# Banded attention output in 64x64 tiles, a re-weighted list schedule, and a reordered first MLP batch

## The chip, the cores and the metric

The kernel runs on one core of one Trainium2 chip. The metric is device time in microseconds (us) of one execution; times given for a kernel are the median of several runs on the chip. The trace is of one profiled execution.

## The reference, cut to what matters

Three stages follow each other on an activation of 4 batches x 576 tokens x 512 channels, all in float32.

```python
# 1. attention over (4, 8 heads, 576, 64): a pooled and a local part, added
q_d, k_d, v_d = mean of q, k, v over groups of 4 tokens         # 144 pooled tokens
out_up = repeat(softmax(q_d @ k_d.T / 8) @ v_d, 4)
mask = abs(pos[:, None] - pos[None, :]) < 4                     # a band of 7 tokens
out_local = softmax(where(mask, q @ k.T / 8, -1e9)) @ v
x = out_up + out_local                                          # heads side by side: 512 channels
# 2. gated MLP with spatial mixing
h = gelu(x @ w_in); u, v = halves of h
v_n = layernorm(v) * g_ln
x = x + (u * (w_sg @ v_n + b_sg)) @ w_out
# 3. four attention experts (causal), top 2 of 4 mixed per token, then the output projection
```

The inputs w_in and w_out arrive as float64 words and are converted to float32 pairs (a high and a low part) on the chip.

## The kernel before, in words

**Stage 1** (function `phase1`) works on 16 units u, each a pair of heads of one batch. The unit's steps carry the names of the list in `unit`:

- `lq`, `lk`, `lv`, `lw`: loads of q, k, v and of ten 64-token windows of v. A q or k load is "whole" (one DMA, six tokens of a head in a run) or split per head (two DMAs of 64-element runs); the table `WHOLE` says for which units.
- `Aq`, `Ak` (TensorE, PE) turn q and k, `aq`, `ak` (ScalarE, ACT) copy them out of PSUM as `qT`, `kT`; `aqd`, `akd` add four neighbouring tokens (VectorE, DVE).
- `Bm` writes the band mask into PSUM, `Bs` adds the local scores (20 matmuls in 64x64 tiles), `Bd` makes the pooled scores. `xm`, `xs`, `sx` (DVE) and `ex` (ACT) are the local softmax, `ym` (DVE) and `ey` (ACT) the pooled one, `n` (DVE) the reciprocals, `ny`, `nx` (GpSimd, POOL) the normalisation, `V` (POOL) the pooled v.
- `Cc`, `Ca` turn the weights, `cb`, `ca` copy them out. `Do` is the banded output: ten matmuls a unit, each with a 128x128 stationary tile `vw` in which the two heads stand on the diagonal and the rest is zero. `Du` is the pooled output; `du` and `dx` add both into `xT`.

The order on every engine is fixed when the program is built: class `Steps` holds each step's engine and cost, its dependencies and a wanted time; `run` takes, among the steps that could start within `NEAR` of the earliest on an engine, the one with the earliest wanted time. PE pays `DRAIN` where a step's tile shape (`mode`) differs from the last one's. An engine executes its list strictly in that order.

Beside the units the same list holds eight conversions of w_in (`conv_job`: a 512 KB load, four DVE operations, one on ACT, three on POOL), five transposes of w_sg (`w_sg_job`), the split of batch 0 into high and low parts (`xhi`, `xlo`) and the first MLP product `du` of batch 0, which is the last thing in it.

**Stage 2** (`phase2`) takes the batches in turn: `dv(b)` (value half, per tile of 128 tokens: PE, then gelu on ACT, `bn_stats` on DVE, the power -0.5 on POOL, the scaling on DVE, and a split on ACT and POOL), `e(b)` (spatial mixing), `dv(b+1)`, `du(b+1)`, `f(b)`. Batch 0's `e` does three column blocks over the first three tiles before it comes to the last ones. Four conversions of w_out run beside it. **Stage 3** (`phase3`) is the mixture of experts; its code is not touched.

Of the kernel before, what the change touches and what calls it, by code (L numbers as in the profile page):

```python
# [8 lines left out]
F32 = mybir.dt.float32  # L9
F32R = mybir.dt.float32r  # L10
# [14 lines left out]
class Steps:  # L25
# [6 lines left out]
    NEAR = 0.4  # L32
# [30 lines left out]
    def run(self):  # L63
        while self.todo:
            can = []
            for name, (engs, fn, want, deps, ring, readers, mode) in self.todo.items():
                t = self.ready(name)
                if t is None:
                    continue
                for e in engs:  # L70
                    x = max(t, self.free.get(e, 0.0))
                    if e == "PE" and mode != self.mode:
                        x += self.DRAIN
                    can.append((x, want, str(name), name, e))
# [18 lines left out]
def tile_pooled_local_attention_gmlp_moe_attention(  # L93
# [32 lines left out]
    TICK = 7.0  # L126
    WHOLE = {"q": lambda u: u < 4, "k": lambda u: u < 10}
# [66 lines left out]
    def phase1():  # L194
        with tc.tile_pool(name="s1", bufs=2, reuse_waits="tile") as p:
            masks = p.tile([P, NP, W], F32, name="masks", bufs=1)
            vws = [p.tile([P, NB, 2, D], F32, name=f"vw{i}", bufs=1) for i in range(3)]
# [10 lines left out]
            for t in vws:  # L208
                for h in range(2):
                    dve.memset(t[64 * h : 64 * h + 64, :, 1 - h], 0.0)  # L210
# [50 lines left out]
            def load_windows(u):  # L261
                b, hp = units[u]
                vw = st.setdefault(u, {})["vw"] = vws[u % 3]
                for h in range(2):
# [3 lines left out]
                        out=vw[r, 1 : NB - 1, h],  # L268
# [3 lines left out]
                        out=vw[r, :: NB - 1, h],  # L272
# [46 lines left out]
            def b_mask(u):  # L319
                t = st[u]["ps"] = wide(f"s{u}")[:, :, : NP * W].rearrange("p h (i w) -> p h i w", w=W)  # L320
                st[u]["psv"] = t.rearrange("p h i w -> p i h w")
                for h in range(2):
                    pe.matmul(t[:, h], identb, mb, start=True, stop=False)
# [28 lines left out]
            def y_max(u):  # L352
# [6 lines left out]
                dve.tensor_scalar(mx, mx, -scale / 16.0, None, op0=ALU.mult)  # L359
# [15 lines left out]
            def n_rec(u):  # L375
                r = st[u]["den"]
                dve.tensor_scalar(r, r, 1e-9, None, op0=ALU.add)
                dve.reciprocal(r, r)

# [34 lines left out]
            def d_po(u):  # L414
# [44 lines left out]
            def unit(u):  # L459
                def do(nm, engs, fn, off, deps, **kw):  # L460
                    args = kw.pop("args", ())
                    steps.add((nm, u), engs, lambda e: fn(u, *args, **({"eng": engines[e]} if nm in ("aq", "ak", "ny", "nx", "cb", "ca") else {})),
                              TICK * u + off, [(d[:-1], u - int(d[-1])) for d in deps.split()
# [4 lines left out]

                do("lq", {"DMA": 1.0 if whole(u, "q") else 1.8}, load, -20.0, "Aq3", args=("q",))
                do("lk", {"DMA": 1.0 if whole(u, "k") else 1.8}, load, -19.0, "Ak3", args=("k",))  # L470
                do("lv", {"DMA": 1.0}, load_v, 0.0, "V2")
                do("lw", {"DMA": 2.0}, load_windows, 14.0, "Do3")
                do("Aq", {"PE": 1.0 if whole(u, "q") else 0.6}, a_pe, 0.0, "lq0", args=("q",), ring="wide",
                   readers=my("aq"), mode=2 if whole(u, "q") else 0)
# [16 lines left out]
                do("ny", {"POOL": 1.2}, n_y, 14.0, "n0")
                do("nx", {"POOL": 1.5}, n_x, 15.0, "n0")
                do("V", {"POOL": 2.2}, stV, 8.0, "lv0 Du3")
                do("Cc", {"PE": 0.7}, c_pc, 19.0, "ny0", ring="wide", readers=my("cb"), mode=0)
                do("Ca", {"PE": 0.6}, c_pa, 19.2, "nx0", ring="wide", readers=my("ca"), mode=0)
                do("cb", {"ACT": 0.9}, c_b, 20.0, "Cc0 Du2")
                do("ca", {"ACT": 0.75}, c_a, 20.2, "Ca0 Do2")
                do("Du", {"PE": 0.5}, d_pu, 26.0, "cb0 V0", ring="narrow", readers=my("du"), mode=2)
# [13 lines left out]
            late = TICK * n  # L512
# [806 lines left out]
```

## Time and profile before

| what | value |
|---|---|
| median of 3 runs | 577.55 us (577.08 to 583.63) |
| profiled execution, its own time | 579.18 us |
| its span, first to last instruction | 577.4 us |
| mean granted TensorE clock | 0.978 of full |
| busy: PE, DVE, ACT, POOL | 538.6, 376.4, 275.8, 236.2 us |

An engine's busy time is the union of its instructions' records; matmuls overlap, so a busy PE may still be waiting inside. "Idle before, releaser" names what an instruction waited for. PEld is the weight load, which runs beside PE. The three stretches that matter are 0 to 160.6 us (the units), 160.6 to 238.3 us (from `du` of batch 0 to the first `f`) and the rest.

### The profile page before, as it was taken

What the parts mean: (1) busy time and instruction counts of PE and PEld (TensorE: products, weight loads), DVE (VectorE), ACT (ScalarE), POOL (GpSimd) and SP (SyncE); (2) the same over time, 40 slices, a digit from 0 to 9 for tenths busy, and PEclk for the clock granted to TensorE, in tenths of its full rate; (3) what the DMA queues carried; (4) which work ended last, traced back from release to release, by engine and by line L of the source; (5) the groups of instructions that cost most, each with busy time, mean ns of one, the idle gap of its engine ahead of it and who ended that gap; (6) DMA issues with size and microseconds to landing.
All of it is one profiled execution on the core that took longest, in us unless ns stands there. A gap on an engine that the chain in (4) does not pass through costs nothing.

```text
span 577.4 us, 12339 instructions
## 1 busy us (share of the span) xinstructions
PE 538.6 (93%) x4723; PEld 485.2 (84%) x4723; DVE 376.4 (65%) x935; ACT 275.8 (48%) x679; POOL 236.2 (41%) x323
## 2 busy tenths in 40 slices
PE   8797998998899779899999999999899899899997
PEld 5776887777798769898999899999889698798875
DVE  7788898999616777164415414626969758768863
ACT  3455464757614333302420240335867656765862
POOL 4675776577203556204401420771324223223430
PEclk9899797999999998999999999999999999999999
DMA  9999779692110202000000000210000010001013
GB/s 231 189 196 198 157 175 186 157 196 59 27 71 2 73 2 56 0 1 1 0 1 1 1 1 1 55 39 1 2 1 2 2 37 37 2 37 56 2 64 102
DMA packets 61146, 34.93 MB, mean 60 GB/s; under 512 B 51296, under 2 KB 53984, under 8 KB 61088
## 3 DMA queue, kind: packets, MB, share of 16 engines
q1 hardware_dynamic: 61088, 34.15, 26.0%
q8 instruction: 37, 0.61, 0.5%
q14 instruction: 21, 0.17, 0.1%
HBM read 29.42 MB, written 4.72 MB: 59 GB/s over the span
## 4 chain that ended last, share of the span: by engine, by line
PE 54%; DVE 20%; issue 8%; POOL 8%; ACT 8%; DMA 3%; SPq 0%; ACTq 0%; DVEq 0%; POOLq 0%
PE f L689 6%; PE e L689 5%; PE v L689 4%; PE wide L421 4%; PE i L689 4%; PE av L1137 4%; PE gq L689 4%; PE dv L689 3%; PE sc L689 3%; PE du L689 3%; PE gk L689 3%; POOL vn L189 3%; PE wide L689 2%; PE tr L1099 2%; DVE vg L741 2%
## 5 line engine op out<-in xcount | busy, mean ns | idle before, releaser
L189 POOL TENSOR_TENSOR gT<-z,gT 128x576 fp32r<-128x576 f32 x16 | 23.4, 1467 | 96.3 <-ACT gT L159 96.3
L689 PE MATMUL e<-wsgT,vn 128*128 128x288 f32 x384 | 56.4, 295 | 1.5 <-POOL vn L189 1.5
L689 PEld LDWEIGHTS e<-wsgT,vn 128*128 128x128 f32 x384 | 52.8, 188 | 1.8 <-POOL vn L189 1.7
L689 PE MATMUL f<-gT,wouts 128*128 128x288 f32 x384 | 51.8, 295 | 0.5 <-POOL gT L189 0.5
L689 PEld LDWEIGHTS f<-gT,wouts 128*128 128x128 f32 x384 | 51.2, 188 | 0.7 <-POOL gT L189 0.7
L689 PE MATMUL dv<-win,xhla 128*128 128x512 f32 x192 | 48.4, 413 | 2.9 <-ACT vg L724 2.9
L159 ACT CAST gT<-z 128x576 fp32r<-128x576 f32 x16 | 10.8, 674 | 81.9 <-DVE z L796 81.9
L821 DVE TENSOR_TENSOR xT<-f,xT 128x576 f32<-128x576 f32 x16 | 12.1, 758 | 56.1 <-PE f L689 56.1
L689 PEld LDWEIGHTS dv<-win,xhla 128*128 128x128 f32 x192 | 37.8, 199 | 12.3 <-ACT vg L724 3.4
L421 PE MATMUL wide<-aTs,vw 128*128 128x58 f32 (+1 forms) x320 | 42.0, 291 | 4.4 <-DVE X L350 4.2
L421 PEld LDWEIGHTS wide<-aTs,vw 128*128 128x128 f32 x320 | 40.5, 207 | 6.6 <-DVE X L350 5.4
L689 PE MATMUL du<-xhla,win 128*128 128x288 f32 x288 | 39.0, 296 | 1.9 <-ACT uT L709 1.9
L689 PEld LDWEIGHTS du<-xhla,win 128*128 128x128 f32 x288 | 38.6, 189 | 2.4 <-ACT uT L709 2.1
L1088 POOL TENSOR_SCALAR xT<-xT,sden,wt 128x128 f32<-128x128 f32 (+3 forms) x32 | 19.6, 612 | 44.5 <-DVE sden L1086 25.1
L689 PE MATMUL gq<-xhlb,w 128*128 128x288 f32 x192 | 30.0, 301 | 6.0 <-DVE smx L1074 2.7
L1088 POOL TENSOR_SCALAR Xs<-Xs,sden,wt 128x128 f32<-128x128 f32 (+3 forms) x32 | 19.6, 612 | 35.5 <-DVE sden L1086 30.6
L689 PEld LDWEIGHTS gq<-xhlb,w 128*128 128x128 f32 x192 | 26.3, 189 | 8.0 <-DVE xhlb L189 3.1
L189 POOL TENSOR_TENSOR vn<-vg,vn 128x512 fp32r<-128x512 f32 x16 | 21.9, 1370 | 20.8 <-ACT vn L159 20.8
L741 DVE TENSOR_SCALAR vg<-vg,mv 128x512 f32<-128x512 f32 x18 | 12.7, 704 | 26.3 <-POOL mv L731 26.3
L689 PE MATMUL gk<-xhlb,w 128*128 128x288 f32 x192 | 27.9, 295 | 0.0
L315 POOL TENSOR_TENSOR vd<-v 72x256 f32<-72x256 f32 x16 | 11.9, 742 | 37.6 <-DMA v<-in_v_dram 15.4
L689 PEld LDWEIGHTS gk<-xhlb,w 128*128 128x128 f32 x192 | 26.6, 188 | 0.7
(199 smaller groups left out, 1390.7 us busy)
## 6 DMA issues: line engine op xcount, KB each, us to landing
v<-in_v_dram SPq DMA_DIRECT2D x16, 288.0 KB
wst<-in_moe_w_in_dram SPq DMA_DIRECT2D x8, 512.0 KB
vw<-in_v_dram SPq DMA_DIRECT2D x32, 128.0 KB
out_dram<-os SPq DMA_DIRECT2D x16, 256.0 KB
q<-in_q_dram SPq DMA_DIRECT2D x24, 144.0 KB
k<-in_k_dram SPq DMA_DIRECT2D x10, 288.0 KB
wst<-in_moe_w_out_dram SPq DMA_DIRECT2D x4, 512.0 KB
k<-in_k_dram SPq DMA_DIRECT2D x12, 144.0 KB
```

Of the source, the lines that this page charges most:

```text
L159: act.copy(o, i)
L189: e_lo.tensor_tensor(lo, src, raw(hi), op=ALU.subtract)
L315: pool.tensor_tensor(vd[:R], vv[:, :, :, 0], vv[:, :, :, 1], op=ALU.add)
L421: pe.matmul(t[:, q0:q1], d["vw"][:, c].rearrange("w h d -> w (h d)"), aTs[:, c // 2, x0 + q0 : x0 + q1], start=True, stop=True)
L689: pe.matmul(o, l, r, start=(first and i == 0), stop=(last and i == n - 1))
L741: dve.tensor_scalar(g, g, mv[:, 0:1], mv[:, 1:2], op0=ALU.subtract, op1=ALU.mult)
L821: dve.tensor_tensor(dst, os_[mt][:, :, :HS], dst, op=ALU.add)
L1088: pool.tensor_scalar(X, X, den, w, op0=ALU.mult, op1=ALU.mult)
L1099: pe.transpose(o[:, j * P : (j + 1) * P], X[:, s0 : s0 + P], ident)
L1137: pe.matmul(o[64 * h : 64 * h + 64, a0 - c0 : c1 - c0], (vs[b][:, j] if j < NT - 1 else vr[b])[:, e * D : (e + 1) * D], rhs, start=(j == 0 ...
```

## The change

1. `Do` uses 20 matmuls of 64x64 tiles a unit, one per head and window; `vw` shrinks to half and its zero blocks go. The mask `Bm` becomes four matmuls on 64x64 tiles.
2. The pooled sum of q moves from DVE to POOL (three additions); the scaling of the pooled maximum and the addition of 1e-9 move from DVE to ACT.
3. A conversion uses one DVE operation less (absolute value on ACT, a clamp on POOL; POOL's addition goes).
4. 5 units load q whole (before 4), 2 load k whole (before 10).
5. New costs, wanted times, `NEAR` 0.2 and a bonus `STAY` for a step that keeps PE's tile shape. The last four conversions of w_in and the w_sg transposes get wanted times behind the units.
6. In `dv`, the previous tile is finished after the current one's statistics; the rest tile comes fourth; batch 1's split is spread over `dv(0)`; the last low part goes to DVE; `e(0)` starts on tiles 0 and 1.

```diff
-    NEAR = 0.4
+    NEAR = 0.2
+    STAY = 3.51
-                    if e == "PE" and mode != self.mode:
-                        x += self.DRAIN
+                    w = want
+                    if e == "PE":
+                        x += self.DRAIN if mode != self.mode else 0.0
+                        w -= self.STAY if mode == self.mode else 0.0
...
-    TICK = 7.0
-    WHOLE = {"q": lambda u: u < 4, "k": lambda u: u < 10}
+    TICK = 6.7
+    WANT = {
+        "lq": -3.2, "lk": -4.6, "lv": 4.3, "lw": 27.5, "Aq": 0.2, "Ak": 0.3, "aq": -9.6, "ak": -18.6,
...
+    WHOLE = {"q": lambda u: u < 5, "k": lambda u: u < 2}
...
-                for h in range(2):
-                    pe.matmul(t[:, h], identb, mb, start=True, stop=False)
+                for g in range(2):
+                    for h in range(2):
+                        r = slice(64 * h, 64 * h + 64)
+                        pe.matmul(t[64 * g : 64 * g + 64, h], identb[r, r], mb[r, g], start=True, stop=False)
...
-                    pe.matmul(t[:, q0:q1], d["vw"][:, c].rearrange("w h d -> w (h d)"),
-                              aTs[:, c // 2, x0 + q0 : x0 + q1], start=True, stop=True)
+                    for h in range(2):
+                        r = slice(64 * h, 64 * h + 64)
+                        pe.matmul(t[r, q0:q1], d["vw"][r, c], aTs[r, c // 2, x0 + q0 : x0 + q1], start=True, stop=True)
...
+                pool.tensor_tensor(t, x[:, :, 0], x[:, :, 1], op=ALU.add)
+                pool.tensor_tensor(ta, x[:, :, 2], x[:, :, 3], op=ALU.add)
+                pool.tensor_tensor(t, t, ta, op=ALU.add)
...
-                dve.tensor_scalar(mx, mx, -scale / 16.0, None, op0=ALU.mult)
+                act.activation(mx, mx, AF.Copy, scale=-scale / 16.0)
-                dve.tensor_scalar(r, r, 1e-9, None, op0=ALU.add)
+                act.activation(r, r, AF.Identity, bias=eps)
...
-            t = 12.0 + 12.5 * i
+            t = 41.6 + 20.4 * i if i < KT else 298.9 + 2.6 * (i - KT)
-            t = 88.0 + 7.0 * i
+            t = 292.4 + 2.9 * i
...
-            dve.tensor_scalar(d["ex"], up, 20, 0x7FF, op0=ALU.logical_shift_right, op1=ALU.bitwise_and)
-            dve.tensor_scalar(d["mn"], up, 3, 0x7FFFF8, op0=ALU.logical_shift_left, op1=ALU.bitwise_and)
+            dve.tensor_scalar(d["mn"], d["ab"].bitcast(I32), 3, 0x3FFFFFF8, op0=ALU.logical_shift_left, op1=ALU.bitwise_and)
-            pool.tensor_tensor(d["mn"], d["mn"], d["ex"], op=ALU.add)
+            act.activation(d["ab"], d["t"][:, :, 1].bitcast(F32), AF.Abs)
+            pool.tensor_scalar(d["ab"], d["ab"], 2.0 ** -15, 2.0 ** -15, op0=ALU.max, op1=ALU.max)
...
-                flush()
                 pool.tensor_scalar(mv[:, 1:2], mv[:, 1:2], 1e-6, None, op0=ALU.add)
                 pool.tensor_tensor(mv[:, 1:2], mv[:, 1:2], neghalf, op=ALU.pow)
+                flush()
...
-                for t in list(range(NT - 1)) + ([NT - 1] if b % 2 == 0 else []):
+                for t in [*range(NT - 2), *([NT - 1] if b % 2 == 0 else []), NT - 2]:
...
-                    for dt in range(3):
-                        part(dt, range(NT - 2))
+                    for ts in (range(2), [2]):
+                        for dt in range(3):
+                            part(dt, ts)
```

PE's list in the middle of the units, before: `q2_0` is unit 8's q, `kd7` the pooled k of unit 7, `vw2` the windows of unit 5.

```order
L340 MATMUL narrow1_161<-kd7_1017,qd7_981 64x144 x6
L284 MATMUL wide1_159<-ident_67,q2_0_748 128x96 x6
L331 MATMUL wide0_158<-kT7_1003,qT7_969 64x64 x20
L282 MATMUL wide_97<-ident_67,k2_0_778 64x96 x12
L434 MATMUL narrow0_160<-bTs1_94,vd2_90 64x144 x4
L401 MATMUL wide1_159<-ident_67,Y6_944 72x128 x6
L421 MATMUL wide0_158<-aTs1_92,vw2_87 128x58 x9
L421 MATMUL wide0_158<-aTs1_92,vw2_87 128x54
L394 MATMUL wide_97<-ident_67,X6_995 128x128 x5
```

The same place after; L445 is `Do`, L347 `Bs`, L356 `Bd`, L457 `Du`, L291 the turns of q and k.

```order
L445 MATMUL wide_95<-aTs1_90,vw0_83 64x58 x18
L445 MATMUL wide_95<-aTs1_90,vw0_83 64x54 x2
L347 MATMUL wide0_145<-kT6_777,qT6_769 64x64 x20
L356 MATMUL narrow0_147<-kd6_790,qd6_797 64x144 x6
L457 MATMUL narrow1_148<-bTs0_91,vd1_87 64x144 x4
L291 MATMUL wide1_146<-ident_67,q2_0_880 128x96 x6
L291 MATMUL wide_95<-ident_67,k2_0_859 128x96 x6
L356 MATMUL narrow1_148<-kd7_915,qd7_907 64x144 x6
```

The full-width `Do` that stood between `Cc` and `Ca` now stands with `Bs` and `Bd`, which have its tile shape, and k is turned in six operations where twelve stood.

POOL's list at the same units, before (Y and X are `ny` and `nx`, vd is `V`, wmn and win a conversion):

```order
L388 TENSOR_TENSOR Y6_944<-Y6_944,den6_943 128x432
L383 TENSOR_TENSOR X6_995<-X6_995,den6_943 128x640
L315 TENSOR_TENSOR vd2_90<-v2_0_1072 72x256
L316 TENSOR_TENSOR vda8_1143<-v2_0_1072 72x256
L317 TENSOR_TENSOR vd2_90<-vd2_90,vda8_1143 72x256
L388 TENSOR_TENSOR Y7_1068<-Y7_1068,den7_1067 128x432
L383 TENSOR_TENSOR X7_1121<-X7_1121,den7_1067 128x640
```

After, qd is the pooled q:

```order
L307 TENSOR_TENSOR qd8_1101<-qT8_1063 128x144
L308 TENSOR_TENSOR qda8_1102<-qT8_1063 128x144
L309 TENSOR_TENSOR qd8_1101<-qd8_1101,qda8_1102 128x144
L329 TENSOR_TENSOR vd1_87<-v1_3_990 72x256
L330 TENSOR_TENSOR vda7_1118<-v1_3_990 72x256
L331 TENSOR_TENSOR vd1_87<-vd1_87,vda7_1118 72x256
L410 TENSOR_TENSOR Y6_988<-Y6_988,den6_987 128x432
L405 TENSOR_TENSOR X6_994<-X6_994,den6_987 128x640
```

POOL now serves a unit at three places of its list: the pooled q at the unit's start, `V` in the middle, `ny` and `nx` late.

POOL's list in `dv(0)`, before (mv the statistics of a tile, vn the low part of the tile):

```order
L731 TENSOR_TENSOR mv0_0_2336<-mv0_0_2336,neghalf_75 128x1
L189 TENSOR_TENSOR vn0_2317<-vg0_0_2333,vn0_2317 128x512
L730 TENSOR_SCALAR mv0_1_2362<-mv0_1_2362 128x1
L731 TENSOR_TENSOR mv0_1_2362<-mv0_1_2362,neghalf_75 128x1
L189 TENSOR_TENSOR vn0_2317<-vg0_1_2356,vn0_2317 128x512
```

After:

```order
L754 TENSOR_TENSOR mv0_0_2511<-mv0_0_2511,neghalf_74 128x1
L753 TENSOR_SCALAR mv0_1_2537<-mv0_1_2537 128x1
L754 TENSOR_TENSOR mv0_1_2537<-mv0_1_2537,neghalf_74 128x1
L198 TENSOR_TENSOR vn0_2492<-vg0_0_2508,vn0_2492 128x512
L753 TENSOR_SCALAR mv0_2_2565<-mv0_2_2565 128x1
L754 TENSOR_TENSOR mv0_2_2565<-mv0_2_2565,neghalf_74 128x1
```

Tile 1's statistics no longer stand behind tile 0's low part. From the first `f(0)` matmul to the end, the lists of all five engines read the same in both kernels.

## Rows read from the trace of the kernel before

**Rows 1.** By stretch: length, busy PE, PEld, DVE, ACT, POOL; clock, DMA share, GB/s.
```profile
0.00:160.60 160.60, 142.19 (x1968) 121.03 (x1969) 134.71 (x225) 88.99 (x221) 99.07 (x126) 0.95 0.78 163
160.60:238.30 77.70, 69.36 (x414) 62.79 (x414) 45.50 (x70) 25.16 (x42) 32.93 (x34) 0.96 0.11 30
```

**Rows 2.** PE in order of time: start us, us, instruction [idle before, releaser].
```profile
10.77 0.75 PE L331 MATMUL wide<-kT,qT 64*64 64x64 f32 x36
...
92.62 0.85 PE L401 MATMUL wide<-ident,Y 128*72 128x128 f32 x6 [1.81 <-ACT qT L159]
94.15 4.15 PE L421 MATMUL wide<-aTs,vw 128*128 128x58 f32 x20
...
146.02 0.81 PE L331 MATMUL wide<-kT,qT 64*64 64x64 f32 x40
```

**Rows 3.** PE groups, 0 to 160.6 us: busy us, mean ns, then idle before.
```profile
L421 PE MATMUL wide<-aTs,vw 128*128 128x58 f32 (+1 forms) x320 | 42.0, 291 | 4.4 <-DVE X L350 4.2 <-ACT aTs L159 0.2
L331 PE MATMUL wide<-kT,qT 64*64 64x64 f32 x640 | 13.9, 223 | 2.1 <-issue 2.1
...
L282 PE MATMUL wide<-ident,k 96*64 96x96 f32 x240 | 13.0, 261 | 0.3 <-DVE xT L446 0.3
...
L284 PE MATMUL wide<-ident,k 96*128 96x96 f32 x36 | 4.2, 254 | 0.0
```

**Rows 4.** DVE groups, 0 to 160.6 us.
```profile
L295 DVE TENSOR_REDUCE qd<-qT 128x144 f32<-128x576 f32 x16 | 11.9, 745 | 1.1 <-ACT qT L159 1.0
...
L377 DVE TENSOR_SCALAR den<-den 128x13 f32<-128x13 f32 x16 | 8.5, 529 | 0.5
L359 DVE TENSOR_SCALAR mx<-mx 128x3 f32<-128x3 f32 x16 | 7.8, 484 | 0.6
L608 DVE TENSOR_SCALAR wmn<-wst 128x512 int32<-128x512 int32 x8 | 6.7, 840 | 0.0
L614 DVE SCALAR_TENSOR_TENSOR wmn<-wst,wmn 128x512 int32<-128x512 int32 x8 | 6.4, 804 | 0.0
L607 DVE TENSOR_SCALAR wex<-wst 128x512 int32<-128x512 int32 x8 | 6.2, 781 | 2.5 <-DMA wst<-in_moe_w_in_dram 2.5
L618 DVE SCALAR_TENSOR_TENSOR wmn<-wst,wmn 128x512 int32<-128x512 int32 x8 | 6.0, 750 | 0.0
...
L210 DVE MEMSET vw<- 64x640 f32 x6 | 3.6, 592 | 0.9 <-issue 0.9
```

**Rows 5.** POOL groups, 0 to 160.6 us.
```profile
L383 POOL TENSOR_TENSOR X<-X,den 128x640 f32<-128x640 f32 x16 | 20.5, 1282 | 0.0
...
L316 POOL TENSOR_TENSOR vda<-v 72x256 f32<-72x256 f32 x16 | 12.4, 777 | 0.0
...
L628 POOL TENSOR_TENSOR win<-wmn,win 128x512 fp32r<-128x512 f32 x8 | 10.2, 1275 | 0.4
L622 POOL TENSOR_TENSOR wmn<-wmn,wex 128x512 int32<-128x512 int32 x8 | 10.2, 1270 | 4.1 <-DVE wmn L618 4.1
L166 POOL TENSOR_SCALAR win<-wmn 128x512 fp32r<-128x512 f32 x8 | 5.0, 620 | 0.4
```

**Rows 6.** ACT group of the small copies, 0 to 160.6 us.
```profile
L441 ACT ACTIVATE up<-narrow 128x144 f32<-128x144 f32 x16 | 4.5, 282 | 0.1
```

**Rows 7.** The stretch with the largest loads, as Rows 1.
```profile
5.00:15.00 10.00, 8.85 (x186) 7.25 (x186) 8.88 (x18) 4.81 (x12) 2.73 (x6) 1.00 1.08 265
```

**Rows 8.** Chain of work later in stage 2: start us, us, what.
```profile
251.04 14.85 PE e L689 x112
265.90 13.99 PE dv L689 x60
279.88 12.74 PE du L689 x96
```

**Rows 9.** POOL in dv(0), in order of time, as Rows 2.
```profile
180.57 1.29 POOL L189 TENSOR_TENSOR vn<-vg,vn 128x512 fp32r<-128x512 f32 x1 [1.31 <-ACT vn L159]
...
184.14 1.56 POOL L189 TENSOR_TENSOR vn<-vg,vn 128x512 fp32r<-128x512 f32 x1 [1.31 <-ACT vn L159]
```

More of the change, by code (lines that the diff above doesn't have):

```diff
@@ L467, in my @@
                     return [(x, u) for x in names]
[L469 to L473, printed above, removed]
+                do("lq", {"DMA": 1.1 if whole(u, "q") else 1.75}, load, "Aq3", args=("q",))
@@ L491, in unit @@
[L491 to L498, printed above, removed]
@@ L499, in unit @@
-                do("Do", {"PE": 1.15}, d_po, 26.1, "ca0 lw0", ring="wide", readers=my("dx"), mode=0)
-                do("du", {"ACT": 0.3}, d_up, 27.0, "Du0 dx2")
-                do("dx", {"DVE": 0.75}, d_x, 28.0, "Do0 du0")
+                do("aq", {"ACT": 0.65}, a_q, "Aq0 Bs2 aqd2")
+                do("ak", {"ACT": 0.65}, a_k, "Ak0 Bs2 akd2")
+                do("aqd", {"POOL": 1.3}, a_qd, "aq0 Bd2")
+                do("akd", {"DVE": 0.76}, a_kd, "ak0 Bd2")
+                do("Bd", {"PE": 0.9}, b_psd, "aqd0 akd0", ring="narrow", readers=my("ym", "ey"), mode=1)
@@ new lines, in unit @@
+                do("Bm", {"PE": 0.36}, b_mask, "aq0 ak0 xs1", ring="wide", readers=my("xm", "xs"), mode=1)
+                do("Bs", {"PE": 0.75}, b_ps, "Bm0", mode=1)
+                do("ym", {"DVE": 0.62}, y_max, "Bd0 xs3 ey3 ny4 nx4 Cc3")
+                do("yb", {"ACT": 0.25}, y_bias, "ym0")
+                do("ey", {"ACT": 1.6}, e_y, "yb0")
+                do("xm", {"DVE": 0.82}, x_max, "Bs0 ym0 Ca3")
+                do("xs", {"DVE": 0.84}, x_sub, "xm0")
+                do("ex", {"ACT": 0.76}, e_x, "xs0")
@@ new lines, in unit @@
+                do("sx", {"DVE": 0.82}, x_sum, "ex0")
+                do("ne", {"ACT": 0.25}, n_eps, "sx0 ey0")
+                do("n", {"DVE": 0.26}, n_rec, "ne0")
+                do("ny", {"POOL": 0.98}, n_y, "n0")
+                do("nx", {"POOL": 1.35}, n_x, "n0")
+                do("V", {"POOL": 2.35}, stV, "lv0 Du3")
+                do("Cc", {"PE": 0.72}, c_pc, "ny0", ring="wide", readers=my("cb"), mode=0)
+                do("Ca", {"PE": 0.57}, c_pa, "nx0", ring="wide", readers=my("ca"), mode=0)
@@ L503, in phase1 @@
+                do("cb", {"ACT": 0.8}, c_b, "Cc0 Du2")
+                do("ca", {"ACT": 0.7}, c_a, "Ca0 Do2")
+                do("Du", {"PE": 0.6}, d_pu, "cb0 V0", ring="narrow", readers=my("du"), mode=2)
+                do("Do", {"PE": 0.75}, d_po, "ca0 lw0", ring="wide", readers=my("dx"), mode=1)
+                do("du", {"ACT": 0.3}, d_up, "Du0 dx2")
+                do("dx", {"DVE": 0.75}, d_x, "Do0 du0")
             for u in range(n):
@@ L824, in phase2 @@
             split_rem(0, "a")
[L825 removed]
+            early = split_x(1, act, dve, "a")
             dv(0)
```

148 lines of the change are left out of this document (72 added, 76 removed), and 4 rows, old and new, of the table WANT.

## Prediction, made before the changed kernel ran

> **What bounds the kernel now.** I read the busy time by stretch first, then the groups of the unit stretch, then PE's timeline, then the chain of waits. The stretches show where anything can be had [rows 1]. The units take 160.6 us, in which PE is busy 142.2 and DVE 134.7, with the DMA engines at a share of 0.78, which is 125 us of work; POOL has 99.1 and ACT 89.0. So no single engine fills the stretch: two are near it, the loads are third, and 18.4 us of PE's time are lost to waits. The next stretch, to the first `f`, takes 77.7 us. From 238.3 us to the end of the 577.4 us span the lists of all engines read the same in both kernels, so I cost those 339.1 us at no change.
>
> PE's timeline gives the pace: the scores of unit 0 start at 10.77 us, those of unit 15 at 146.02 [rows 2], which is 135.25 / 15 = 9.02 us a unit, and `du` follows at 160.6, 14.6 us behind the last scores. PE also does not keep its clock: after an idle 1.81 us at 92.62 one `Do` takes 4.15 us [rows 2], against 42.0 / 16 = 2.6 in the mean [rows 3], and over the whole stretch the granted clock averages 0.95 [rows 1], between the levels 1.2 and 2.4 GHz.
>
> **The change, part by part: the units.** I add up each engine's work and then ask how closely it can be packed.
>
> *PE.* `Do` costs 42.0 us for 16 units, the dearest group by far: 20 instructions of 128x58 a unit [rows 3]. It becomes 40 instructions of 64x58. The trace has no such instruction. The nearest is `Bs`, also 40 a unit in 64x64 tiles: 13.9 / 16 = 0.87 us [rows 3]. The other end is the unpaired 64-wide turn of k, 13.0 us for 240 or 54 ns each [rows 3], which makes 40 x 54 = 2.2 us. `Bs` goes round four tiles and `Do` only alternates between two, so I take 1.0, near the low end: 42.0 - 16 = 26 us less (20 to 28 by the ends 1.4 and 0.87 that I think possible; 7 by the far one). Eight k turned split instead of whole save 1.30 - 0.70 each [rows 3], 4.8 us; one q goes the other way, +0.6. The mask's four matmuls for two I take at nothing, between -0.2 and +0.3 us a unit. About 2 us of w_sg turns leave. PE: 142.2 - 26 - 4.8 + 0.6 - 2 = 110 us.
>
> *DVE* loses the pooled q (11.9), the addition to the sums (8.5), the scaling (7.8) and the clears of `vw` (3.6), all by [rows 4]. A conversion costs 6.2 + 6.7 + 6.4 + 6.0 = 25.3 us for eight [rows 4]; four remain, with three operations of about 0.8 each, 9.6 us. 134.7 - 31.8 - 15.7 = 87 us.
>
> *ACT* gets both small operations: 32 at the price of its smallest copy, 0.28 us [rows 6], 9 us. 89.0 + 9 = 98; 0.2 to 0.5 each makes it 95 to 105. They also put ACT into two chains that it was not in, the pooled softmax and the reciprocals, behind copies of 0.6 to 0.8 us.
>
> *POOL* gets three additions of 144 elements a unit. By its two nearest rows an element costs 1282 / 640 = 2.0 or 777 / 256 = 3.0 ns [rows 5]; 0.43 us each, by the row nearer in length, makes 48 x 0.43 = 20.6 us (14 to 37, the latter if an operation cannot be shorter than 0.78). Eight conversions cost 10.2 + 5.0 + 10.2 = 25.4; four remain, at 1.28 + 0.62 and a clamp of 0.62, 10.1 us. 99.1 + 20.6 - 15.3 = 104 us.
>
> *DMA.* In the stretch with the largest pieces 265 GB/s stand at a share of 1.08 [rows 7], so 245 GB/s full. Of the 26.2 MB in the units' stretch (163 GB/s x 160.6 us) 15.7 come in large pieces by the sizes of the loads, 64 us; the 10.5 MB in pieces of 64 elements take the other 61 us, 172 GB/s. A split load of 0.295 MB then costs 1.72 us for 1.20. Seven more of them: +3.6. Four conversions' loads leave (8.6), and two of w_out and three of w_sg by their 1.9 MB (8). 125 + 3.6 - 16.6 = 112 us.
>
> So 142, 135, 125, 99, 89 become 110, 87, 112, 104, 98. The largest goes from 142 to 112. At the same ratio the stretch would be 112 x 160.6 / 142 = 127 us; with the same loss, 112 + 18 = 130. I expect more loss, since three resources now stand within 8 us of each other instead of two, and a pooled q makes PE's `Bd` wait for POOL, behind which its list has `V` and the normalisations of older units. I take 25: **137 us**, that is a pace of 7.5 us a unit (10.8 + 15 x 7.5 + 14). By the ends of the prices it is 124 (110 of PE at the old ratio) to 151 (a `Do` of 2.2 and a mask of +0.3 us, PE 134, with a loss of 17). Saved: 23.6 us.
>
> **The change, part by part: the first MLP batch.** The work of PE between `du` and the first `f` is, by later batches [rows 8], 12.7 + 14.0 + 14.9 + 4/5 of 14.0 + 12.7 = 65.5 us; 77.7 are taken, so 12 are lost. POOL's timeline shows why: the low parts of tiles 0 and 1 start at 180.57 and 184.14 [rows 9], 3.6 us apart where PE needs 14.0 / 5 = 2.8 a tile, because the next tile's statistics stand behind the low part. In the new order they stand ahead of it, and `e(0)` has tiles 0 to 2 to work on while the last tile is finished. I let 4 of the 12 us stay, for `dv(1)` has w_out's conversions beside it. Three w_sg turns are now here, 15 matmuls at 4.2 / 36 = 0.12 [rows 3], +2. And the value half of w_in is converted here, where it was hidden in the units: load 2.1, ACT 0.7, clamp 0.62, DVE 2.4, high 0.62, low 1.28, 7.7 us through, and POOL's 2.5 for each of three more: 15.2 us beside `du`'s 12.7 + 2. That hides if the four loads start with `du`; the last two wait for the buffers of the first two, so I add 3 (0 to 8). 65.5 + 4 + 2 + 3 = 74.5: saved 3 (from 8 saved to 6 lost).
>
> **The sum.** 579.18 - 23.6 - 3 = 552.6 by the profiled execution, which lies 1.6 above the median of the runs and 1.8 above its own span; I say 552.
>
> **Rivals.**
> *The two heads do not overlap.* The alternating tiles of `Do` write into one PSUM bank. If they go one by one at the 54 ns of the unpaired turn [rows 3], `Do` takes 2.2 us a unit, PE 110 + 19 = 129 us, and PE is the bound again at 129 + 20 = 149: 579.2 - 11.6 - 3 = 565. For it speaks that no row shows 58 columns in two tiles; against it that `Bs` gets 13.9 us / 640 = 22 ns an instruction. Chance 0.13.
> The Trainium skill, TensorEngine Tiling (Array Packing), section Restrictions and Gotchas, says that different row tiles cannot access the same PSUM bank simultaneously. `Bs` has its two row tiles in different banks, so its row does not contradict that; no row here shows `Do` either way. By that rule this rival holds, and without it the 1.0 us of my sum.
> *The conversions moved behind come back.* If the value half's chain runs one by one, `dv(0)` waits 10 us more, and PE, idle for that long, comes back at the lower clock: 552.6 + 10 = 563. For it speaks that the loads of the last two stand behind others in DVE's list; against it that `du` covers 14.7 us. 0.11.
> *The loads set the pace.* The issue queue is in order too, and a load waits there for its buffer; at a DMA share of 0.72 in place of 0.78 the units need 112 / 0.72 = 156 us: 579.2 - 4.6 - 3 = 572. For it speaks a share of 1.08 early on [rows 7]; against it the smaller sum. 0.11.
> *POOL becomes the bound with its waits.* It is idle 160.6 - 99.1 = 61.5 us now, 3.8 a unit [rows 1]. If the pooled q, which the scores need, only adds a further place to wait, and the 3.8 stay on top of 104 / 16 = 6.5, the pace is 10.3 us and the units take 11 + 154 + 14 = 179: 579.2 + 18.4 - 3 = 595, slower. It decides once the pace passes 9.2 us. For it speaks that POOL's list now has a unit's early step between late steps of older units; against it that most of its idle time now is waiting for others' slower pace. 0.07.
>
> **How the numbers follow.** The forecast has 0.58, with its own range 541 to 565. A measurement of this kernel tells about 2% from no change, so faster means below 566. The forecast and the second rival count as faster nearly whole, the first by two thirds, the third by a third: 0.56 + 0.10 + 0.08 + 0.04 = 0.78; slower is the last rival, 0.07; the rest, 0.15, is the same. The range 539 to 572 leaves out the slow rival and a unit stretch packed better than 124.
>
> **What would show it.** Right: `du` of batch 0 starts at 130 to 144 us; the group of `Do` has about 16 us; DVE's busy time in the units is under 95 and POOL's over 100; low parts in `dv(0)` follow each other in under 3.2 us. Wrong: a `Do` over 1.6 us a unit at full clock; POOL idle before the pooled q or PE idle before `Bd` for most units; a granted clock below 0.85 in the units; PE idle by more than 6 us before `dv(0)`; or any gain or loss after the first `f`.

## The result, and the profile after

| | before | changed |
|---|---|---|
| median of the runs | 578.94 us (577.08 to 583.63, 4 runs) | 554.63 us (552.79 to 555.84, 4 runs) |
| profiled execution, its span | 579.18, 577.4 us | 555.15, 553.1 us |

The ratio is 0.957 with a 95% interval of 0.950 to 0.963: faster by 4.3%. The prediction said 552. Some runs of a kernel go at a lower granted clock and take over 1.5% longer than its fastest; ratios leave them out, and so does the median of do_wide below (568.56 and 569.20 us of its four runs). The stretches of the changed kernel, in the columns of [rows 1]: the units, and from `du` of batch 0 to the first `f`.

```profile
0.00:136.84 136.84, 115.01 (x2178) 97.26 (x2178) 92.40 (x139) 87.33 (x239) 114.19 (x162) 0.95 0.95 176
136.84:212.19 75.35, 71.34 (x427) 64.97 (x428) 53.62 (x90) 30.73 (x56) 45.96 (x43) 0.95 0.17 50
```

The units went from 160.6 to 136.84 us, 23.8 less, and the next stretch from 77.7 to 75.35. What follows took 340.9 us for 339.1. Almost the whole gain is in the units, where the DMA engines now stand at a share of 0.95, and POOL and PE are level.

PE in order of time, the scores of the first and the last unit and a `Do` followed by the next step (compare [rows 2]):

```profile
11.07 0.75 PE L347 MATMUL wide<-kT,qT 64*64 64x64 f32 x36
...
122.83 0.76 PE L347 MATMUL wide<-kT,qT 64*64 64x64 f32 x38
...
134.54 1.37 PE L445 MATMUL wide<-aTs,vw 64*64 64x58 f32 x40
135.84 0.77 PE L671 MATMUL wide<-ident,wsg 128*128 128x128 f32 x5
```

(122.83 - 11.07) / 15 = 7.45 us a unit for 9.02. The 40 records of a `Do` take 1.30 us from start to next start, 33 ns each. The groups of the units, to set beside [rows 3] to [rows 6]: PE's, the new POOL steps with `X` for scale, the conversion's and the two small steps of ACT.

```profile
L445 PE MATMUL wide<-aTs,vw 64*64 64x58 f32 (+1 forms) x640 | 24.0, 229 | 4.1 <-ACT up L464 2.4 <-DMA vw<-in_v_dram 1.1 <-ACT qT L170 0.2
...
L405 POOL TENSOR_TENSOR X<-X,den 128x640 f32<-128x640 f32 x16 | 20.1, 1258 | 0.0
...
L347 PE MATMUL wide<-kT,qT 64*64 64x64 f32 x640 | 16.5, 233 | 0.8 <-issue 0.8
...
L633 POOL TENSOR_SCALAR wab<-wab 128x512 f32<-128x512 f32 x6 | 11.5, 1922 | 5.1 <-ACT wab L630 5.1
...
L309 POOL TENSOR_TENSOR qd<-qd,qda 128x144 f32<-128x144 f32 x16 | 8.7, 546 | 1.3
...
L307 POOL TENSOR_TENSOR qd<-qT 128x144 f32<-128x144 f32 x16 | 7.6, 475 | 5.1 <-ACT qT L170 5.1
L308 POOL TENSOR_TENSOR qda<-qT 128x144 f32<-128x144 f32 x16 | 7.6, 473 | 0.0
...
L640 DVE SCALAR_TENSOR_TENSOR wmn<-wst,wmn 128x512 int32<-128x512 int32 x5 | 5.7, 1131 | 0.1
...
L400 ACT ACTIVATE den<-den,eps 128x13 f32<-128x13 f32 x16 | 4.9, 306 | 3.4 <-DVE den L392 3.2
...
L378 ACT ACTIVATE mx<-mx 128x3 f32<-128x3 f32 x16 | 3.3, 209 | 6.9 <-DVE mx L374 6.9
```

`Do`'s group fell from 42.0 to 24.0 us. The clamp of a conversion, L633, is the surprise: 1.92 us each, three times the 0.62 us of the copy of the same size [rows 5].

### The profile page after: what moved, and what is told of

Read it like the earlier page. It is cut to its first block, busy times and chain, and to the rows that moved or that the text cites. A ratio compares the mean times of both kernels' runs of the same rounds, so it can differ in the third digit from the quotient of the medians.

```text
span 553.1 us, 12748 instructions
## 1 busy us (share of the span) xinstructions
PE 514.5 (93%) x4949; PEld 464.6 (84%) x4949; DVE 345.6 (62%) x872; ACT 280.2 (51%) x711; POOL 263.1 (48%) x365
## 4 chain that ended last, share of the span: by engine, by line
PE 52%; POOL 14%; DVE 12%; issue 8%; ACT 7%; DMA 5%; SPq 1%; DVEq 0%; POOLq 0%; ACTq 0%
PE e L713 7%; PE f L713 6%; PE v L713 5%; PE i L713 4%; PE gq L713 4%; PE av L1167 4%; PE sc L713 3%; PE gk L713 3%; PE dv L713 3%; POOL vn L198 3%; DMA v<-in_v_dram 2%; PE wide L713 2%; PE tr L1129 2%; PE wide L445 2%; DVE bst L751 2%
## 5 line engine op out<-in xcount | busy, mean ns | idle before, releaser
L713 PE MATMUL e<-wsgT,vn 128*128 128x288 f32 x384 | 58.9, 302 | 2.3 <-ACT vn L170 2.2
L713 PEld LDWEIGHTS e<-wsgT,vn 128*128 128x128 f32 x384 | 54.9, 193 | 3.0 <-ACT vn L170 2.5
L713 PE MATMUL dv<-win,xhla 128*128 128x512 f32 x192 | 45.6, 394 | 1.5 <-ACT uT L733 0.8
L713 PEld LDWEIGHTS dv<-win,xhla 128*128 128x128 f32 x192 | 35.7, 188 | 10.0 <-POOL win L651 2.1
L751 DVE BATCH_NORM_STATS2 bst<-vg 128x6 f32<-128x512 f32 x18 | 12.5, 693 | 25.0 <-ACT vg L748 24.7
L445 PE MATMUL wide<-aTs,vw 64*64 64x58 f32 (+1 forms) x640 | 24.0, 229 | 4.1 <-ACT up L464 2.4
L445 PEld LDWEIGHTS wide<-aTs,vw 64*64 64x64 f32 x640 | 22.1, 144 | 6.5 <-ACT up L464 2.5
L633 POOL TENSOR_SCALAR wab<-wab 128x512 f32<-128x512 f32 x12 | 24.7, 2057 | 6.0 <-ACT wab L630 6.0
L713 PE MATMUL i<-w,yT 128*128 128x512 f32 x96 | 25.6, 400 | 0.0
```

The lines of the kernel that those rows point to most:

```text
L445: pe.matmul(t[r, q0:q1], d["vw"][r, c], aTs[r, c // 2, x0 + q0 : x0 + q1], start=True, stop=True)
L633: pool.tensor_scalar(d["ab"], d["ab"], 2.0 ** -15, 2.0 ** -15, op0=ALU.max, op1=ALU.max)
L713: pe.matmul(o, l, r, start=(first and i == 0), stop=(last and i == n - 1))
L751: dve.bn_stats(stt, g)
```

## The experiments

All twelve, each timed beside the kernel before. "du" is the start of `du` of batch 0 in the profiled run, the end of the units; "clock" is the granted clock up to there (1.00 is 2.4 GHz, 0.50 is 1.2 GHz).

| kernel | median us | ratio to before, 95% | du | clock |
|---|---|---|---|---|
| changed kernel | 554.63 | 0.950 to 0.963 | 136.8 | 0.95 |
| do_tiles_alone | 575.61 | 0.980 to 0.994 | 153.1 | 0.94 |
| dve_relief_alone | 597.36 | 1.018 to 1.033 | 175.4 | 0.84 |
| do_tiles_and_dve_relief | 578.62 | 0.995 to 1.001 | 157.3 | 0.93 |
| do_wide | 559.90 (two runs) | 0.952 to 0.969 | 141.1 | 0.98 |
| old_wants | 562.44 | 0.957 to 0.975 | 141.7 | 0.90 |
| do_two_banks | 553.25 | 0.944 to 0.956 | 134.6 | 0.95 |
| no_windows | 553.73 (one run) | | 134.3 | 0.95 |
| clamp_dve | 554.95 | 0.945 to 0.962 | 138.6 | 0.91 |
| qd_dve | 553.19 | 0.945 to 0.959 | 134.5 | 0.96 |
| loads_and_pool_cut | 539.73 (one run) | | 122.9 | 1.00 |
| dv_old | 552.80 | 0.943 to 0.960 | 139.4 | 0.94 |
| wout_old_slots | 564.04 | 0.963 to 0.975 | 133.4 | 0.96 |

Three of these, the changed kernel, dv_old and wout_old_slots, have the same list on every engine up to du, and their du differs by 6 us (133.4 to 139.4). So a single du says nothing about 3 us. The kernels were timed in four groups, and the kernel before had a median of 579 to 582 us in them; so two kernels of different groups are compared by their ratios as well as by their medians.

**Parts of the change in the kernel before.** First `Do` alone:

```diff
-    pe.matmul(t[:, q0:q1], d["vw"][:, c].rearrange("w h d -> w (h d)"), aTs[:, c // 2, ...], ...)
+    for h in range(2):
+        r = slice(64 * h, 64 * h + 64)
+        pe.matmul(t[r, q0:q1], d["vw"][r, c], aTs[r, c // 2, ...], ...)
```

> The kernel before with one part of the change: Do in 64x64 tiles, vw of half the size, the clears of vw gone; orders, engines and loads as before. Theory A (the small Do is what shortens the units, whatever else is done): PE loses some 18 us of work (42.0 to 24 us) and the stretch follows, du of batch 0 starts near 143 and the time is near 561. Theory B (DVE, with 131 us left, was as near the bound as PE, and the old order leaves its waits where they are): du starts near 153 to 158 and the time is 570 to 575, so the rest of the change is needed for the gain.

Measured: du at 153.1, 7.5 us less for 18 us less of `Do`, 1.3% of the time. That is Theory B, with 575.6 us just above its range.

Then the three small DVE jobs alone, at their old places in the lists:

```diff
-    dve.tensor_reduce(t, x, axis=AX.X, op=ALU.add)
+    pool.tensor_tensor(t, x[:, :, 0], x[:, :, 1], op=ALU.add)
+    pool.tensor_tensor(ta, x[:, :, 2], x[:, :, 3], op=ALU.add)
+    pool.tensor_tensor(t, t, ta, op=ALU.add)
-    dve.tensor_scalar(mx, mx, -scale / 16.0, None, op0=ALU.mult)
+    act.activation(mx, mx, AF.Copy, scale=-scale / 16.0)
-    dve.tensor_scalar(r, r, 1e-9, None, op0=ALU.add)
+    act.activation(r, r, AF.Identity, bias=eps)
```

> The kernel before with another part of the change alone: the pooled q in three additions on POOL, the scaling of the pooled maximum and the addition of 1e-9 on ACT, all at their old places in the lists; Do in 128x128, conversions, loads and order as before (the ten warming matmuls 384 columns wide for the room). DVE falls from 134.7 to about 107 us in the units, PE stays at 142. Theory K (PE and DVE bound the units together, so relieving one alone gives part): du of batch 0 starts at 150 to 156 instead of 160.6, time 567 to 574. If PE alone was the bound: 158 to 161, time 575 to 580.

Both expectations missed, with the other sign: 2.6% slower. Its units, and its waits up to 150 us (engine, step, releaser: us in total, times, longest):

```profile
0.00:175.40 175.40, 157.52 (x1967) 137.09 (x1968) 114.65 (x177) 94.03 (x253) 123.14 (x175) 0.84 0.71 152
```

```profile
ACT mx L368 <- DVE mx L367: 18.4, 10, 4.2
POOL qd L302 <- ACT qT L159: 17.5, 8, 5.4
DVE den L387 <- ACT den L386: 15.4, 11, 4.4
```

DVE did lose 20 us of work (134.7 to 114.65), but each of the three steps, put on another engine at its old place, waits there for its input or makes the next one wait: 51 us of waits on three engines. Not all of it is new; in the kernel before ACT waited at the first of these places for DVE's scaling:

```profile
ACT Y L367 <- DVE mx L359: 8.8, 9, 2.3
```

PE was not idle for longer: 175.4 - 157.52 = 17.9 us, 18.4 before. The whole 14.8 us are in its busy time, by the clock: a mean of 0.84 means that a third of the stretch, 56 us, went at 1.2 GHz, where 0.95 before makes about 17 us. These 39 us more at half speed are worth some 20 us of PE's work, an estimate, so at the old clock the moves might have gained. PE's waits were fewer and longer (up to 3.2 us, 2.1 before), and `Do` ran slow behind them, as here after a wait for POOL's normalisation:

```profile
74.85 1.50 PE L410 MATMUL wide<-ident,Y 128*72 128x128 f32 x6 [2.65 <-POOL Y L397]
76.15 4.35 PE L430 MATMUL wide<-aTs,vw 128*128 128x58 f32 x20
```

In the changed kernel, to 134 us, the same three waits are 14.5 us:

```profile
ACT mx L378 <- DVE mx L374: 6.9, 5, 4.8
...
POOL qd L307 <- ACT qT L170: 5.1, 2, 3.7
...
DVE den L396 <- ACT den L400: 2.5, 3, 1.8
```

Both in one kernel:

> Both parts in the kernel before: Do in 64x64 tiles and the three small DVE jobs moved, order, conversions and loads as before. PE has 127 us and DVE 103 in the units. Theory K: the two together give more than Do's 7.5 us alone, du at 141 to 147 and the time 560 to 566; the rest down to 136.8 is the new order's and the late conversions'. Rival (the old order and eight early conversions hold the pace): du at 149 to 153, time 568 to 573.

Measured: du at 157.3 and no difference that can be told from the kernel before. Its units:

```profile
0.00:157.28 157.28, 128.46 (x2287) 104.12 (x2288) 116.25 (x171) 93.48 (x253) 124.41 (x175) 0.93 0.84 169
```

Theory K falls in this order of the work, and du lies beyond the rival's range too: the largest sum fell from 142 to 128 us and the stretch by 3.3. PE's idle time rose from 18.4 to 28.8 us; its largest wait, up to 150 us, is for POOL's normalisation, in this kernel and in the one before:

```profile
PE wide L407 <- POOL Y L394: 9.8, 5, 3.8
...
PE wide L401 <- POOL Y L388: 3.9, 3, 2.0
```

**Parts taken back from the changed kernel.** `Do` in 128x128 again (the diff of do_tiles_alone the other way):

> The changed kernel with Do back at ten matmuls of a 128x128 stationary tile, in the same place of every list (vw of full size, with its clears; the ten warming matmuls are 448 instead of 512 columns wide for the room). PE's work in the units rises by 18 us, from 115 to 133. Theory A (PE sets the pace): du of batch 0 starts near 155 and the time is near 572. Theory C (the loads, at a share of 1.0 up to 120 us, set the pace, and PE has 22 us free): PE takes most of it from its idle time, du starts at 140 to 146 and the time is 558 to 564.

```profile
0.00:141.14 141.14, 128.53 (x1858) 111.95 (x1858) 95.52 (x145) 87.73 (x239) 115.14 (x162) 0.98 0.92 170
```

PE took 13.5 us more of work and the stretch 4.3; by the ratios `Do`'s tiles are worth 2 us here and by the medians 5, with intervals that overlap. That is Theory C's size, not Theory A's 18: PE takes 9 us of the work out of its idle time (21.8 to 12.6 us), and by this row it also kept its clock better (0.98 for 0.95). Theory C's reason, that the loads set the pace, does not hold by itself, as no_windows shows below.

The wanted times and list rules of before:

```diff
-    NEAR = 0.2; STAY = 3.51; TICK = 6.7
+    NEAR = 0.4; STAY = 0.0; TICK = 7.0
-    "lq": -3.2, "lk": -4.6, ..., "Bs": -18.4, ..., "ny": -21.1
+    "lq": -20.0, "lk": -19.0, ..., "Bs": 7.3, ..., "ny": 14.0
```

> The changed kernel with the wanted times of the units' steps, TICK, NEAR and STAY of the kernel before (the two new small steps wanted half a microsecond ahead of the ones they were cut from); the late conversions stay late. If the gain in the units comes from the work taken off PE and DVE: du starts within 3 us of 136.8 and the time is 552 to 559. If it comes from the new order: du starts at 146 to 155, time 564 to 573.

```profile
0.00:141.71 141.71, 122.78 (x2179) 101.95 (x2179) 93.03 (x139) 88.03 (x238) 111.53 (x161) 0.90 0.85 170
141.71:220.68 78.97, 71.92 (x430) 64.19 (x428) 55.88 (x90) 31.13 (x57) 48.65 (x44) 0.96 0.16 48
```

Measured: du at 141.7, and 8 us by the medians or 5.5 by the ratios, between the two expectations. The three other kernels of its group have 552.8 to 555.0. So the new order is worth 5 to 8 us. In the profiled run 4.9 lie in the units, 2.3 beyond the range of equal lists, and 3.6 in the stretch behind them. Again PE was not idle for longer (18.9 us for 21.8); its busy time rose by 7.8 us with the clock at 0.90.

The units' 23.8 us thus come in three steps: 3.3 from `Do`'s tiles and the moves at their old places, 15.6 from there to old_wants, 4.9 from the new order. The middle step, the largest, is late and shorter conversions, late w_sg turns, the other loads, the mask in tiles and lists built with the moved steps on their new engines. No run takes these apart.

**What sets the pace now.** Three kernels take one piece of work away, from the loads or from POOL, and one takes all:

```diff
@@ load_windows, no_windows
+                if u > 2:
+                    return
@@ clamp, clamp_dve
-            pool.tensor_scalar(d["ab"], d["ab"], 2.0 ** -15, 2.0 ** -15, op0=ALU.max, op1=ALU.max)
+            dve.tensor_scalar(d["ab"], d["ab"], 2.0 ** -15, 2.0 ** -15, op0=ALU.max, op1=ALU.max)
@@ pooled, qd_dve
-                if eng is dve:
+                if True:
                     dve.tensor_reduce(t, x, axis=AX.X, op=ALU.add)
```

loads_and_pool_cut has all three.

> The changed kernel with the loads of v's windows left out from unit 3 on (Do then works on the windows of units 0 to 2, so this leaves 13 of 16 window loads out). Some 4.3 MB in small pieces go, about 27 us of the DMA engines' 130. Theory C (the loads set the pace): du of batch 0 starts at 120 to 127 instead of 136.8. Theory F (PE, POOL and the waits between them set it, POOL being busy for 114 of 136.8 us): du starts at 134 to 137.

> The changed kernel with the clamp of the conversions on DVE instead of POOL, at the same place of the program. POOL loses five to six times 1.92 us in the units (114 to 104 us), DVE gains five or six times 0.7 us at most (92 to 96). Theory G (after the change POOL, busy for 114 of 136.8 us, sets the pace of the units): du of batch 0 starts at 127 to 131 and the time is 545 to 550. Theory H (no single engine sets it, each unit's chain of steps does): du starts at 135 to 137, time 552 to 555.

> The changed kernel with the pooled q back on DVE (one addition over four, 0.74 us), at the same place. POOL loses 16 x 1.5 = 24 us (114 to 90), DVE gains 12 (92 to 104), PE stays at 115. Theory G (POOL sets the pace): du starts at 120 to 126, PE becoming the bound, and the time is 540 to 548. Theory I (moving the pooled q off DVE is what the change needs, since DVE is in the softmax chain): du starts at 141 to 148, time 558 to 566. Theory H: du starts at 135 to 138.

> The changed kernel with the window loads left out from unit 3 on (Do works on the windows of units 0 to 2), and the pooled q and the clamp on DVE. DMA has some 103 us of work, POOL 80, DVE about 107, PE 115. Theory J (loads and POOL each hide behind the other and behind PE, so that cutting one alone showed 2 us): du starts at 122 to 130. Theory H (the waits that the fixed lists make between the engines, and PE's own 115 us, are what is left): du starts at 132 to 137.

Measured: one by one du comes at 134.3, 138.6 and 134.5, all within the 6 us that equal lists differ by, and the two ratios with an interval do not differ from the changed kernel's. The units of no_windows, clamp_dve and qd_dve:

```profile
0.00:134.27 134.27, 114.17 (x2178) 96.83 (x2178) 94.27 (x139) 87.84 (x239) 113.66 (x162) 0.95 0.72 147
...
0.00:138.62 138.62, 118.31 (x2178) 100.49 (x2178) 93.81 (x144) 87.22 (x239) 103.56 (x156) 0.91 0.90 174
...
0.00:134.52 134.52, 114.19 (x2178) 96.26 (x2178) 98.26 (x155) 87.47 (x239) 92.28 (x114) 0.96 0.94 179
```

With the windows cut POOL still has 113.7 us of work; with the pooled q off POOL the DMA engines still have 0.94 x 134.52 = 126 us. PE's waits up to 134 us changed sides too: for POOL's pooled q in no_windows (1.2 us in the changed kernel), for the loads of windows in clamp_dve (1.1 us there) and of q in qd_dve (0.6 us there):

```profile
PE narrow L358 <- POOL qd L311: 3.4, 3, 1.9
...
PE wide L445 <- DMA vw<-in_v_dram: 4.8, 4, 2.2
...
PE wide L291 <- DMA q<-in_q_dram: 4.6, 2, 2.5
```

Together du comes at 122.9, 14 us earlier, and the time is 539.7:

```profile
0.00:122.89 122.89, 109.08 (x2179) 91.96 (x2179) 100.25 (x160) 88.00 (x240) 82.49 (x108) 1.00 0.75 161
```

Theory C, Theory G and Theory I fall, Theory H falls with the last run, Theory J stands. Loads and POOL each hide behind the other; with both cut PE is left with 109 of 122.9 us, at the full clock, 5.9 us less busy and 8.0 us less idle than in the changed kernel. This rests on one run, whose 122.9 lies 10.5 us below the lowest du of equal lists. Not run is a kernel with both POOL steps cut and the loads left; that the loads have to go as well is read from qd_dve's DMA share and waits. In the kernel before, too, no single relief gave its own size, but there the two together did not either.

**Does `Do` wait at a bank?** Head 1 follows by five windows, so neighbours never share a bank:

```diff
-    t = d["po"] = wide(f"o{u}").rearrange("c a s -> c (a s)")[:, 512 % QB :]
+    t = d["po"] = wide(f"o{u}").rearrange("c a s -> c (a s)")[:, 512 - 5 * QB :]
...
     for c in range(NB):
         for h in range(2):
+            w = (c + 5 * h) % NB
...
-            pe.matmul(t[r, q0:q1], d["vw"][r, c], aTs[r, c // 2, x0 + q0 : x0 + q1], start=True, stop=True)
+            pe.matmul(t[r, q0:q1], d["vw"][r, w], aTs[r, w // 2, x0 + q0 : x0 + q1], start=True, stop=True)
```

> The changed kernel, result and work the same, but head 1's windows follow head 0's by five and the tile starts elsewhere, so that two neighbouring matmuls of Do never write into the same PSUM bank. Theory D (different row tiles wait for each other at one bank): Do falls from 1.31 us a unit (33 ns a record) to about 0.9 (22 ns, as the scores, which have their row tiles in two banks); the time falls by 0 to 4 us, since PE is not alone at the bound. Theory E (the loads of the stationary tiles set the 33 ns): Do stays at 1.3 us a unit, and so does the time (554 to 556).

```profile
L446 PE MATMUL wide<-aTs,vw 64*64 64x58 f32 (+1 forms) x640 | 24.4, 231 | 2.6 <-DMA vw<-in_v_dram 2.0 <-ACT qT L170 0.3
```

24.4 us for 24.0, 231 ns for 229: Theory D falls. That the loads of the stationary tile set the 33 ns (Theory E) agrees with this, but no run changed them.

**The first MLP batch.** The order of dv and e as before (and the split of batch 1 all ahead of dv(0)):

```diff
     act.activation(g, o, AF.Gelu_apprx_tanh)
+    flush()
...
-    flush()
...
-    split(vn[b][:, 0, t], vn[b][:, 1, t], g, act, dve if last else pool)
+    split(vn[b][:, 0, t], vn[b][:, 1, t], g, act, pool)
...
-    for t in [*range(NT - 2), *([NT - 1] if b % 2 == 0 else []), NT - 2]:
+    for t in list(range(NT - 1)) + ([NT - 1] if b % 2 == 0 else []):
...
-    for ts in (range(2), [2]):
-        for dt in range(3):
-            part(dt, ts)
+    for dt in range(3):
+        part(dt, range(NT - 2))
```

> The changed kernel with dv, the split of batch 1, the last low part and e of batch 0 in the order of the kernel before; units and conversions stay as changed. The forecast gave this reordering about 8 of the 12 us that PE lost there, against 5 us for the late conversions and w_sg turns. If so, du of batch 0 still starts at 137 and the first f 6 to 9 us later than in the changed kernel, at 218 to 221, time 560 to 564. Rival (the low part's loop paces dv at 4 us a tile either way, as the profile after still shows): first f at 212 to 215, time 554 to 557.

Measured: 74.95 us from du to the first `f` for 75.35, and 552.80 us for 554.63; the other kernels with the new order of dv and e and the late w_out took 73.7 to 75.3, old_wants apart. The reordering is worth nothing that shows.

The places of w_out's conversions as before:

```diff
-    jobs[(0, 1, 6, 7)[kk]] = [conv_job(...)]
+    jobs[(0, 1, 3, 4)[kk]] = [conv_job(...)]
...
-    [fetch, lambda: None] + [lambda: None] * (i < 2 * KT + 2) + [size, clamp, bits, lambda: (stt1(), stt2()), lambda: (hi_(), lo_())]
+    [fetch, lambda: None, lambda: (size(), clamp(), bits()), lambda: (stt1(), stt2()), lambda: None, lambda: (hi_(), lo_())]
```

> The changed kernel with the conversions of w_out in the places that they had before (starts 0, 1, 3, 4 and no later stages), so that three of them fall beside e of batch 0 and dv of batch 1. Theory L (the gain of the first MLP batch is that dv(1) no longer waits behind w_out's conversions): dv(1) takes 14 to 17 us instead of 11.0, the first f comes 78 to 81 us after du instead of 75.4, time 556 to 561. Rival (it is dv(0)'s order or the freed DVE): 74 to 76 us, time 552 to 555.

Measured: 84.8 us for 75.35, and 9.4 us by the medians or 7 by the ratios, more than expected in this stretch, but not in dv(1), which took 11.9 us. PE's waits in this stretch, and POOL and DVE ahead of the longest:

```profile
PE e L713 <- ACT vn L170: 6.4, 1, 6.4
PE du L713 <- ACT uT L733: 2.8, 1, 2.8
```

```profile
170.62 1.93 POOL L633 TENSOR_SCALAR wab<-wab 128x512 f32<-128x512 f32 x1
```

```profile
165.85 0.43 DVE L637 TENSOR_SCALAR wmn<-wab 128x512 int32<-128x512 int32 x1 [3.97 <-POOL wab L633]
...
172.58 0.43 DVE L637 TENSOR_SCALAR wmn<-wab 128x512 int32<-128x512 int32 x1 [3.06 <-POOL wab L633]
172.93 0.75 DVE L198 TENSOR_TENSOR xhla<-xT,xhla 128x576 fp32r<-128x576 f32 x1
173.60 0.69 DVE L751 BATCH_NORM_STATS2 bst<-vg 128x6 f32<-128x512 f32 x1
```

DVE waits 3.97 and 3.06 us for a clamp with dv(0)'s statistics queued behind, so two tiles of dv(0) come later. Theory L is right in kind (the places of w_out's conversions decide) and wrong in place.

## Why the prediction was right, point by point

The total and both stretches came out as forecast (137 and 136.84; 74.5 and 75.35). That several sums close together bound the units held. But the closeness of the two numbers is luck: in each stretch two errors cancelled, as the points on the packing and on the MLP reordering show. Of the signs set out, the group of `Do` at about 16 us and the low parts under 3.2 us did not come.

- *Sums of work.* PE 115 for 110; the 40 records of `Do` take 1.3 us at full clock for 1.0, as a group 24.0 us for 16, and `Bs` grew to 16.5 us. DVE 92 for 87: its conversion steps took 0.8 to 1.1 us, not 0.8, and five conversions ran there, not four. POOL 114 for 104: six clamps of 1.92 us where I had four of 0.62, and 23.9 us of pooled q for 20.6. ACT 87 for 98: I had not taken off the w_sg copies and conversion steps that leave, 5 of the 11 us. The mis-sized term is the DMA's: 0.95 x 136.84 = 130 us for 112. Leaving 4.3 MB of windows out took 130 - 0.72 x 134.27 = 33 us, 128 GB/s, where I had 172 for small pieces. And six loads of w_in and nearly all of w_sg still fall into the units, 1.75 MB that I had taken out, which is an estimated 7 of the 18 us at my 245 GB/s.
- *The packing.* My 25 us of loss on 112 us came out because the largest sum was really 130 and the loss on it 7: luck in the number. The reason given, several resources close together, is what loads_and_pool_cut shows.
- *The new order.* I gave it no price of its own and priced the moves at their durations. That step failed: the same moves at their old places cost 15 us alone and 4 on top of `Do`'s tiles (157.3 for 153.1), alone by the clock, with the tiles mostly by PE's waits for POOL. Rival 4, POOL with its waits, named the mechanism in part: there du came at 175.4 where the rival had 179. In the changed kernel it stays away mostly by what old_wants already has, du at 141.7, with another 4.9 us by the new order.
- *The two heads do not overlap.* The rival's price did not come: 33 ns a record, not the 54 of the unpaired turn [rows 3]. Whether the heads overlap no run shows, since a turn has 96 columns and `Do` 58, and 54 x 58 / 96 is 33 too. The Trainium skill, TensorEngine Tiling (Array Packing), section Restrictions and Gotchas, has different row tiles unable to access one PSUM bank simultaneously; here one bank or two made no difference (229 and 231 ns).
- *The conversions come back.* In the changed kernel PE waits 0.7 us for them in dv(0), where I had 3. But the last of w_out now ends behind the first `f`, which takes 13.9 us for 12.7 before; this is most of the 1.8 us lost where I had no change:

```profile
213.77 0.40 PE L713 MATMUL f<-gT,wouts 128*128 128x288 f32 x1 [0.22 <-ACT wouts L170]
214.49 11.73 PE L713 MATMUL f<-gT,wouts 128*128 128x288 f32 x86 [0.32 <-DVE wouts L651]
```

- *The loads set the pace.* The share is higher than that rival had, and yet the loads alone decide nothing.
- *The MLP reordering.* "I let 4 of the 12 us stay" failed as a reason: the 8 us that it gives the reordering did not come (dv_old), and 6 us that no term held came in dv(1), which is luck. POOL's low parts in dv(0) follow at 4.0 us, not under 3.2, as the loop is still closed: the next tile's gelu waits for the last low part.

```profile
163.31 0.60 ACT L748 ACTIVATE vg<-dv 128x512 f32<-128x512 f32 x1 [0.83 <-POOL vn L198]
```

```profile
161.98 1.30 POOL L198 TENSOR_TENSOR vn<-vg,vn 128x512 fp32r<-128x512 f32 x1
...
166.02 1.29 POOL L198 TENSOR_TENSOR vn<-vg,vn 128x512 fp32r<-128x512 f32 x1
```

The gain is in dv(1): 17.1 us before, 11.0 after. There the second half waited for a gelu in the kernel before:

```profile
206.20 5.76 PE L689 MATMUL dv<-win,xhla 128*128 128x512 f32 x24
214.90 8.56 PE L689 MATMUL dv<-win,xhla 128*128 128x512 f32 x24 [2.94 <-ACT vg L724]
223.29 9.72 PE L689 MATMUL du<-xhla,win 128*128 128x288 f32 x72
```

```profile
188.04 11.15 PE L713 MATMUL dv<-win,xhla 128*128 128x512 f32 x48
199.03 9.72 PE L713 MATMUL du<-xhla,win 128*128 128x288 f32 x72
```

The first half's records ended at 211.96, PE stood for 2.94 us, and the second half took 8.39 us to its successor for 5.5, at a mean granted clock of 0.64. du(0) with its w_sg turns and the conversion (+2.7), dv(0) and e(0) (+2.7) and du(1) (-1.7) make up the rest of the 2.4. What made that wait stays open. By the lists it would be w_out's conversions, which stand beside dv(1) in the kernel before and later in the changed one; but with their old places alone dv(1) takes 11.9 us (wout_old_slots), and with the old order of dv alone 11.0 (dv_old). Neither brings the 17.1 back.

## What to carry to other kernels

When two or three engines are within a tenth of each other, price relief by relieving them together; here single cuts gave at most 8 us of their 10 to 33, and one a loss, while loads and POOL together gave 14. A step that is moved to another engine at its old place can cost more than it saves, 15 us here; read PE's idle time and its clock apart, since a loss may lie in the clock alone. And before a small conversion step goes beside a latency chain, measure the step itself.

## What the hardware showed that was not expected

- POOL took 1.92 us for `tensor_scalar` with max and max on 128x512 float32, and 0.62 us for mult and mult of the same size. The clamp works in place and the copy does not; no run shows whether the operation or the place counts.
- Equal lists of instructions on all engines gave units of 133.4, 136.8 and 139.4 us, with clocks of 0.96, 0.95 and 0.94. What starts the difference no run shows.
- In dve_relief_alone PE was busy for 157.5 us with the instructions that took 142.2 in the kernel before. Its idle time was the same (17.9 us for 18.4), in fewer and longer waits; the mean clock fell from 0.95 to 0.84, and the whole loss lies there.
